# Batch 0's kv taken straight from the loaded v, and batch 2's transposes moved to the DMA engines

## The chip, the cores and the metric

The kernel runs on one NeuronCore of a Trainium2 chip. The core has a matrix engine (TensorE, PE in the profile, with its weight loads shown as PEld), VectorE (DVE), ScalarE (ACT), GpSimd (POOL) and SyncE (SP), each working through a queue of its own in program order, and 16 DMA engines that all queues share. The metric is the device time of one execution in microseconds. Before the change the median of 14 runs was 296.78 us (296.46 to 298.65).

## The reference

Linear attention over 8 batches, 8 heads, 576 rows and a head size of 64, and behind it a feed-forward layer with a Swish of its own slope per column:

```python
def phi(x):
    return np.where(x > 0, x, np.exp(x) - 1.0) + 1.0
q_p, k_p = (phi(q), phi(k))
kv = np.einsum('bhsd,bhse->bhde', k_p, v)
z = np.sum(k_p, axis=2)
num = np.einsum('bhsd,bhde->bhse', q_p, kv)
den = np.einsum('bhsd,bhd->bhs', q_p, z)[..., None] + 1e-06
x = (num / den)                  # heads joined: 4608 rows of 512
h = x @ w_in                     # 512 to 2048
g = h * (1.0 / (1.0 + np.exp(-beta * h)))
out = g @ w_out                  # 2048 to 512
```

All inputs are float32 in memory; the kernel converts to bfloat16 when it loads. The output is float32.

## The kernel before

One batch is one stage. A batch's 576 rows are four blocks of 128 and a tail of 64; the tails of all batches are gathered in `xT_tail` and go through the feed-forward layer together as a ninth batch at the end. The order of all work is written out by hand: each engine executes its instructions in the order in which the program names them.

The attention of a batch b has these steps. `load_k`, `load_q` and `load_v` (L81 to L88) load with conversion from GpSimd's queue. `exp_` (L225, ScalarE), `relu` (L233, VectorE) and `phi` (L240, VectorE) give phi(q) and phi(k) in the tile `qk_p`. `v_copy` (L323) copies v into `vaug`, whose columns past the 64 of a head hold ones, so that one matmul, `kv_mm` (L330), gives kv and the sum z together. `kv_evac` (L346) brings them from the accumulators into block-diagonal tiles `kv_bd`. `q_trans` (L369) transposes phi(q) with TensorE and copies the result into `q_pT`. `num_mm` (L390) multiplies a block of it with kv. `num_norm` (L401) divides by the denominator and leaves the tile `xs`; `x_trans` (L423) transposes that with TensorE into `xT`, by a copy of VectorE or ScalarE. For the batches from `DMA_T` on (`by_dma`, L218) two things are different: `q_trans_dma` (L382) transposes all of phi(q) in one transfer from SyncE's queue, and `num_norm` itself issues a transposing transfer of each `xs` on that queue (L414).

The feed-forward layer of a batch has `h_phase` (L455), which makes h in groups (a column block ff, from row block t0 to t1) with a SiLU on ScalarE after each, and `y_phase` (L513) or `y_phase_wide` (L545), which makes the output. Both take a plan: a table of which attention steps of the next batch stand behind which group. `y_phase_wide(b)` goes through ff 0 to 11 for four row blocks at once (plan indices 0 to 11) and then finishes block after block (12 to 15). `h_last` makes the last four column blocks in other accumulators, with ScalarE steps of the next batch between their matmuls and their SiLUs. Accumulators are of two kinds: four banks `mm` and two double banks `att`.

Batch 0 has its own start, written out at L578 to L661, since everything waits for it. It divides the 576 rows into 9 groups (j) of 64 and places heads 0 to 3 in partitions 0 to 63 and heads 4 to 7 in partitions 64 to 127 (`nine`, `load_nine`). `exp0`, `relu0`, `phi0`, `q_trans0`, `q_out0`, `kv_mm0` and `kv_evac0` are the steps above for this layout; `warm` (L565) issues matmuls whose result isn't used.

Around the second place, batch 2's attention stands in `y_phase_wide(1)` (L705 to L716): phi(k) and phi(q) at index 1, kv at 6, the transposes of q at 7 to 9, num_mm and num_norm at 9 to 13, the transposes of x at 11 to 14 and the tail's in `h_phase(2)`. GpSimd's queue holds the loads of later batches (`load_next`); a load of k or q waits until exp and relu of the batch whose buffer it takes are done.

## Time and profile before

| what | value |
|---|---|
| median of 14 runs | 296.78 us (296.46 to 298.65) |
| profiled execution | 297.56 us |
| its span | 295.7 us, 4721 instructions |
| TensorE busy | 284.4 us (96%) |
| VectorE, ScalarE busy | 126.7 us (43%), 175.1 us (59%) |
| DMA packets | 69206, 36.43 MB, mean 123 GB/s |
| mean granted clock | 0.998 |

The profile is one execution. Line numbers are those of the kernel before. Times within the span count from its start. A row of the timeline has the start, the time taken by the row's instructions together, the engine, the line, the operation, what it writes and reads, the size, the count, and in brackets how long the engine had been idle and what ended that. A row of the waits has the engine and line that waited, what it waited for, the total in us, the number of times and the longest. A row of the DMA issues has what is written and read, the queue, the operation, the count, the size of one and the median time from issue to landing.

### The profile page before, as it was taken

Reading aid. Unit: us, or ns where it says so; the run is one execution under the profiler, and the core shown is the slowest. Engines: PE = TensorE matmul, PEld = TensorE weight load, DVE = VectorE, ACT = ScalarE, POOL = GpSimd, SP = SyncE. Lnnn points to the kernel's source line nnn. Section 1 sums busy time; section 2 is a strip of 40 time slices with the busy share of each in tenths; the row PEclk is TensorE's granted clock in tenths of the full one; section 3 lists DMA queues with packets and bytes.
Section 4 is the critical chain, followed back from the end, with each engine's and each line's share of the span. In section 5 each row is a group of like instructions: output and inputs, shape, how many; then the busy total and the mean of one; then the engine's idle time right before and its main releaser. Section 6 shows DMA issues by size and latency. Waiting matters only on the chain.

```text
span 295.7 us, 4721 instructions
## 1 busy us (share of the span) xinstructions
PE 284.4 (96%) x1876; PEld 144.5 (49%) x1897; DVE 126.7 (43%) x267; ACT 175.1 (59%) x232; POOL 50.8 (17%) x72
## 2 busy tenths in 40 slices
PE   8589999999999999999999999999999999999994
PEld 3357446644555454445444544454445444444443
DVE  4686478504673164616461647154715400110012
ACT  2689796889988780778087907790770077018500
POOL 8825565334006000230020000000000000000000
PEclk9999999999999999999999999999999999999999
DMA  7999999999939943799357255024502400020032
GB/s 104 196 207 345 256 272 191 257 193 190 154 124 162 181 94 100 130 171 150 104 124 82 74 115 125 2 71 115 124 2 72 118 35 0 35 91 17 0 72 72
DMA packets 69206, 36.43 MB, mean 123 GB/s; under 512 B 37808, under 2 KB 63680, under 8 KB 69184
## 3 DMA queue, kind: packets, MB, share of 16 engines
q0 software_dynamic: 38400, 20.45, 47.5%
q1 hardware_dynamic: 30624, 15.55, 20.4%
q8 instruction: 15, 0.25, 0.3%
q10 hardware_dynamic: 160, 0.13, 0.2%
q14 instruction: 7, 0.06, 0.1%
HBM read 36.71 MB, written 9.44 MB: 156 GB/s over the span
## 4 chain that ended last, share of the span: by engine, by line
PE 70%; DMA 22%; ACT 2%; issue 2%; POOL 1%; DVE 0%; POOLq 0%
PE mm L448 33%; PE mm L500 32%; DMA xqk<-in_q_dram 9%; DMA xqk<-in_k_dram 6%; DMA w_in<-in_moe_w_in_dram 4%; DMA vraw<-in_v_dram 4%; PE att L394 2%; PE att L339 1%; PE mm L532 1%; ACT e L228 1%; ACT g L440 1%; POOL xqk L132 1%; POOL w_in L160 0%; ACT L228 0%; ACT L573 0%
## 5 line engine op out<-in xcount | busy, mean ns | idle before, releaser
L440 ACT ACTIVATE g<-mm,beta_c 128x512 bf16<-128x512 f32 (+2 forms) x156 | 97.5, 633 | 88.3 <-PE mm L448 88.1
L500 PE MATMUL mm<-w_out,g 128*128 128x512 bf16 x541 | 127.2, 379 | 1.2 <-issue 0.3
L448 PE MATMUL mm<-xT,w_in 128*128 128x512 bf16 (+2 forms) x560 | 108.0, 349 | 0.8 <-DVE xT L365 0.8
L448 PEld LDWEIGHTS <-w_in 128*128 128x128 bf16 x656 | 62.2, 98 | 61.7 <-issue 1.0
L500 PEld LDWEIGHTS <-g 128*128 128x128 bf16 x560 | 52.8, 98 | 57.3
L510 DVE COPY y_sb<-mm 128x512 f32<-128x512 f32 x27 | 18.7, 691 | 70.6 <-PE mm L500 65.6
L228 ACT ACTIVATE e<-xqk 128x2560 bf16<-128x2560 bf16 x14 | 31.9, 2329 | 0.1
L410 DVE TENSOR_TENSOR xs<-att,rden 128x512 bf16<-128x512 f32 (+1 forms) x40 | 27.6, 689 | 1.4
L241 DVE TENSOR_TENSOR qk_p<-r,e 128x2560 bf16<-128x2560 bf16 x14 | 20.9, 1491 | 14.0 <-ACT e L228 13.4
L350 DVE CAST kv_bd<-att 64x130 bf16<-64x130 f32 x28 | 8.2, 292 | 35.1 <-PE att L339 34.8
L72 POOL DMA_DIRECT2D vraw<-in_v_dram x7 | 6.4, 910 | 77.0 <-DVE vaug L365 71.0
L408 DVE TENSOR_SCALAR den<-att 128x8 f32<-128x8 f32 (+1 forms) x40 | 6.4, 161 | 26.9 <-PE att L394 26.7
L394 PEld LDWEIGHTS <-q_pT 128*128 128x128 bf16 (+1 forms) x160 | 11.7, 100 | 10.4 <-DVE xs L410 2.1
L394 PE MATMUL att<-kv_bd,q_pT 128*128 128x130 bf16 (+1 forms) x160 | 15.8, 221 | 0.7 <-DVE kv_bd L365 0.4
L448 PE MATMUL mm<-xT_tail,w_in 128*128 128x512 bf16 x63 | 13.9, 379 | 0.1
L236 DVE TENSOR_SCALAR r<-xqk 128x2560 bf16<-128x2560 bf16 x14 | 11.8, 848 | 4.0 <-DMA xqk<-in_q_dram 2.5
L567 PE MATMUL mm<-g 128*128 128x512 bf16 x35 | 9.8, 434 | 1.2 <-DVE g L144 1.2
L228 ACT ACT_TABLE_LOAD x7 | 9.0, 1283 | 0.1
L409 DVE RECIPROCAL rden<-den 128x8 f32<-128x8 f32 (+1 forms) x40 | 8.1, 201 | 1.4
L72 POOL DMA_DIRECT2D xqk<-in_k_dram x7 | 6.2, 890 | 10.7 <-ACT e L228 5.3
L255 ACT ACTIVATE e<-xqk 128x1280 bf16<-128x1280 bf16 (+1 forms) x4 | 4.4, 1157 | 6.1 <-DMA xqk<-in_k_dram 6.0
L72 POOL DMA_DIRECT2D xqk<-in_q_dram x7 | 6.6, 940 | 8.4 <-DMA xqk<-in_k_dram 5.4
(72 smaller groups left out, 142.9 us busy)
## 6 DMA issues: line engine op xcount, KB each, us to landing
out_dram<-y_sb SPq DMA_DIRECT2D x28, 256.0 KB, 2.3
xqk<-in_k_dram POOLq DMA_DIRECT2D x7, 512.0 KB, 10.8
xqk<-in_q_dram POOLq DMA_DIRECT2D x7, 512.0 KB, 12.4
vraw<-in_v_dram POOLq DMA_DIRECT2D x7, 512.0 KB, 11.6
w_in<-in_moe_w_in_dram POOLq DMA_DIRECT2D x4, 512.0 KB, 10.1
g<-in_moe_w_out_dram POOLq DMA_DIRECT2D x4, 512.0 KB, 10.7
out_dram<-y_sb SPq DMA_DIRECT2D x14, 128.0 KB, 5.2
xqk<-in_moe_w_out_dram POOLq DMA_DIRECT2D x2, 512.0 KB, 13.7
```

What stands on the lines that cost most here:

```text
L72: eng.dma_start(out=dst[:, :, 0:NJ, :].rearrange("p h j d -> p h (j d)"), in_=src[b, :, 0:MAIN, :].rearrange("h (p j) d -> p h (j d)", j=NJ),)
L228: nc.scalar.activation(st[b, "e", a][:, h0:h1], xqk[b % NX][:, a, h0:h1], ACTF.Exp)
L236: nc.vector.tensor_scalar(st[b, "r", a][:, h0:h1], xqk[b % NX][:, a, h0:h1], 0.0, 1.0, ALU.max, ALU.add)
L241: nc.vector.tensor_tensor(st[b, "p"][:, a].rearrange("p j (h d) -> p h j d", h=H)[:, h0:h1], st[b, "r", a][:, h0:h1], st[b, "e", a][:, h0: ...
L350: nc.vector.tensor_copy(kv_bd[b % 2][i][gs, :, g, :], st[b, "kvp"][gs, 2 * i : 2 * i + 2, :])
L394: nc.tensor.matmul(nps[:n, p // 2, c0 : c0 + 2 * (D + 1)], st[b, "qT"][:, t, p, :n], kv_bd[b % 2][p // 2][:, p % 2], start=True, stop=True ...
L410: nc.vector.tensor_mul(xs[:n], nv[:, :, :, 0:D], rden[:n, :, :, None].to_broadcast([n, 2, 4, D]))
L440: nc.scalar.activation(g_sb[b % 2][:, ff, c0:c1], hp[:, c0:c1], ACTF.Silu, scale=beta_c[:, ff : ff + 1],)
L448: nc.tensor.matmul(hp[:, c0:c1], w_in_sb[ff // 4][:, kc, (ff % 4) * P : (ff % 4 + 1) * P], x[:, t0:t1, kc, :] if b < B else x[:, kc, c0:c1 ...
L500: nc.tensor.matmul(yp, g_sb[b % 2][:, ff, t * P : (t + 1) * P], w_out_sb[ff // 4][:, ff % 4, :], start=(ff == 0), stop=(ff == FC - 1),)
L510: nc.vector.tensor_copy(y_sb, yp)
L567: nc.tensor.matmul(st["warm"], g_sb[0][:, FC - 1, 0:P], g_sb[0][:, FC - 1, :], start=True, stop=True, skip_group_check=True,)
```

## The change

In batch 0, kv_mm0 takes v as it was loaded, without the copy and its column of ones. The sums z are made by matmuls of their own, which multiply phi(k) with a tile of two columns of ones and write one column per head of the same accumulators. The loads of v are divided by row group (j below 6, then the rest) instead of by head. phi(q) of the later row groups is made in two pieces, the third q block is transposed before the first h groups, and the others, with their copies, move to other places of the plan and partly from VectorE to ScalarE. `DMA_T` becomes 2, so batch 2's phi(q) and its attention output are transposed by DMA. In batch 2, exp, relu and phi of q come before those of k, and the transfer is issued between phi of q and phi of k. `h_phase(2)` begins with six column blocks in halves (row blocks 0 and 1, then 2 and 3) instead of four.

```diff
-    DMA_T = 3
+    DMA_T = 2
...
-    load_nine(v9, v, h1=2)
-    load_nine(v9, v, h0=2)
+    load_nine(v9, v, j1=6)
+    load_nine(v9, v, j0=6)
...
-    nc.vector.memset(va9[:, :, :, D : D + 2], 1.0)
-    set_ones(1)
+    for i in range(2):
+        set_ones(i)
+    ones = consts.tile([P, 2], BF16)
+    nc.vector.memset(ones, 1.0)
...
-    def v_copy0(h0, h1):
-    def kv_mm0(a, kvp):
...
+    def kv_cols(kvp, g, a):
+        m0 = a * 2 * (D + 1)
+        return kvp[g][:, m0 : m0 + 2 * (D + 1)].rearrange("p (i e) -> p i e", i=2)
+
+    def kv_mm0(kvp, j0, j1, of_v):
+        for j in range(j0, j1):
+            for a in range(2):
+                for g in range(2):
+                    gs = slice(g * TAIL, (g + 1) * TAIL)
+                    cols = kv_cols(kvp, g, a)
+                    nc.tensor.matmul(
+                        cols[:, :, 0:D] if of_v else cols[:, :, D],
+                        st["p0"][1][gs, j, 2 * a : 2 * a + 2, :],
+                        v9[gs, 2 * a : 2 * a + 2, j, :] if of_v else ones[gs],
...
     phi0(0, 0, 4)
-    v_copy0(0, 2)
+    kvp = [mm_bank([P, 512]) for _ in range(2)]
+    kv_mm0(kvp, 0, N9, False)
     qb = att_banks(BF16)
     q_trans0(0, qb, 0)
     q_trans0(1, qb, 256)
-    kvp = [mm_bank([P, 512]) for _ in range(2)]
-    kv_mm0(0, kvp)
     q_out0(0, qb, 0, False)
     q_out0(1, qb, 256, False)
-    warm(1)
-    v_copy0(2, HH)
-    kv_mm0(1, kvp)
+    kv_mm0(kvp, 0, 6, True)
+    kv_mm0(kvp, 6, N9, True)
     kv_evac0(kvp)
...
     num_norm(0, 0)
+    phi0(0, 4, 6)
     warm(4)
     x_trans(0, 0, dve=True)
-    phi0(0, 4, N9)
+    qb2 = att_banks(BF16)
+    q_trans0(2, qb2, 0)
+    q_out0(2, qb2, 0, False)
     num_norm(0, 1)
+    phi0(0, 6, N9)
...
+    def q_rest0():
         q_trans0(3, qb2, 256)
-        q_out0(2, qb2, 0, False)
-        st["qb2"] = qb2
+        q_trans0(4, qb2, 512)
+        q_out0(3, qb2, 256, False)
+        q_out0(4, qb2, 512, False)
...
-            1: [F(q_second)],
-            3: [F(x_trans, 0, 1, dve=True), F(num_mm, 0, 2), F(num_norm, 0, 2),
-                lambda: q_out0(3, st["qb2"], 256, False)],
+            3: [F(x_trans, 0, 1), F(num_mm, 0, 2), F(num_norm, 0, 2), F(q_rest0)],
             5: [F(num_mm, 0, 3), F(num_norm, 0, 3)],
-            6: [F(q_tail0)],
             7: [F(x_trans, 0, 2)],
-            9: [F(x_trans, 0, 3)],
-            10: [F(num_mm, 0, 4), F(num_norm, 0, 4), F(tidy0)],
-            14: [F(x_trans, 0, 4)],
+            8: [F(num_mm, 0, 4), F(num_norm, 0, 4)],
+            9: [F(x_trans, 0, 3), F(tidy0)],
+            12: [F(x_trans, 0, 4)],
...
-            8: [F(begin, 2), F(relu, 2, 1)],
-            10: [F(relu, 2, 0)],
+            8: [F(begin, 2), F(relu, 2, 0)],
+            10: [F(relu, 2, 1)],
...
-    h_last(1, xT[1], [F(exp_, 2, 1), F(exp_, 2, 0)])
+    h_last(1, xT[1], [F(exp_, 2, 0), F(exp_, 2, 1)])
...
-        1: [F(phi, 2, 1), F(phi, 2, 0)],
+        1: [F(phi, 2, 0), F(q_trans_dma, 2), F(phi, 2, 1)],
         6: [F(kv_mm, 2), F(kv_evac, 2)],
-        7: [F(q_trans, 2, 0, 1, wide=True, dve=True)],
-        8: [F(q_trans, 2, 2, 3, wide=True, dve=True)],
-        9: [F(q_trans, 2, 4, wide=True, dve=True), F(num_mm, 2, 0), F(num_norm, 2, 0)],
+        9: [F(num_mm, 2, 0), F(num_norm, 2, 0)],
         10: [F(num_mm, 2, 1), F(num_norm, 2, 1)],
-        11: [F(num_mm, 2, 2), F(num_norm, 2, 2), F(x_trans, 2, 0, wide=True)],
-        12: [F(num_mm, 2, 3), F(num_norm, 2, 3), F(x_trans, 2, 1, wide=True)],
-        13: [F(num_mm, 2, 4), F(num_norm, 2, 4), F(x_trans, 2, 2, wide=True)],
-        14: [F(x_trans, 2, 3, wide=True)],
+        11: [F(num_mm, 2, 2), F(num_norm, 2, 2)],
+        12: [F(num_mm, 2, 3), F(num_norm, 2, 3)],
+        13: [F(num_mm, 2, 4), F(num_norm, 2, 4)],
...
-                [(ff, 0, 2) for ff in range(4)] + [(ff, 2, 4) for ff in range(4)] + ALL[4:]
+                [(ff, 0, 2) for ff in range(6)] + [(ff, 2, 4) for ff in range(6)] + ALL[6:]
             )
-            plan = {1: [F(x_trans, 2, 4)]}
```

## The prediction

> **What bounds the kernel now.** I read the page's busy times and slices first, then TensorE's idle times, then the order of time around the two places that the diff touches, and last the DMA issues. Busy times and slices of the page before:
>
> ```profile
> PE 284.4 (96%) x1876; PEld 144.5 (49%) x1897; DVE 126.7 (43%) x267; ACT 175.1 (59%) x232; POOL 50.8 (17%) x72
> ...
> DMA  7999999999939943799357255024502400020032
> ```
>
> TensorE (PE) is the bound: what leaves its queue is gained, what makes it wait is lost. The DMA row is saturated for about the first 11 slices of 7.4 us, to about 81 us. TensorE's idle times are short; the first belongs to batch 0's start, the second to ScalarE's copies in batch 2:
>
> ```profile
> PE att L281 <- DVE qk_p L269: 2.5, 1, 2.5
> ...
> PE att L394 <- ACT xT L367: 0.3, 1, 0.3
> ```
>
> Batch 0's start, TensorE in order of time. The two rows of L304 are the kv matmuls; between them TensorE waits for the second copy of v:
>
> ```profile
> 12.26 0.41 PE L281 MATMUL att<-identity,qk_p 64*128 64x64 bf16 x16 [2.53 <-DVE qk_p L269]
> 12.63 0.69 PE L304 MATMUL mm<-vaug,qk_p 64*128 64x130 bf16 x18
> 13.58 0.69 PE L304 MATMUL mm<-vaug,qk_p 64*128 64x130 bf16 x18 [0.25 <-issue]
> ```
>
> Batch 2's attention, TensorE; the rows of L375 and L428 are the transposes that the change hands to the DMA engines:
>
> ```profile
> 73.91 0.82 PE L339 MATMUL att<-vaug,qk_p 128*64 128x65 bf16 x40
> 74.89 0.81 PE L500 MATMUL mm<-w_out,g 128*128 128x512 bf16 x3 [0.16 <-issue]
> 75.54 0.61 PE L375 MATMUL att<-identity,qk_p 128*128 128x128 bf16 x8
> 75.98 1.03 PE L500 MATMUL mm<-w_out,g 128*128 128x512 bf16 x4
> ...
> 78.47 0.40 PE L394 MATMUL att<-kv_bd,q_pT 128*128 128x130 bf16 x4
> ...
> 81.19 0.40 PE L428 MATMUL att<-identity,xs 128*128 128x128 bf16 x4
> ...
> 86.69 1.04 PE L448 MATMUL mm<-xT,w_in 128*128 128x256 bf16 x8
> ```
>
> The DMA issues of the page. The 128 KB stores take over twice as long as the 256 KB ones; eight of the fourteen are batch 0's, issued at 49 to 54 us beside the loads (5.2 to 5.6 us each there). The q transposes of batches 3 to 7 take 4.9 us on a queue that is nearly empty:
>
> ```profile
> out_dram<-y_sb SPq DMA_DIRECT2D x28, 256.0 KB, 2.3
> ...
> out_dram<-y_sb SPq DMA_DIRECT2D x14, 128.0 KB, 5.2
> ...
> q_pT<-qk_p SPq DMA_TRANSPOSE x5, 4.9
> ```
>
> **Part A, batch 0.** Both v copies leave VectorE (0.69 and 0.45 us, 12.13 to 13.24 us). The 36 kv matmuls then follow the 16 transposes without a gap: pairs at 0.057 us in the rows above, so 18 pairs from 12.63 us end at 13.8 instead of 14.27 us, 0.45 us earlier. They need the v loads: issued from 4.70 us, 5.6 to 6 us to landing each, so the last at about 12.45 us, before the matmuls of j 6 to 8 at 13.3 us. The 36 new sum matmuls, two columns each, start at phi(k)'s first half (10.4 us); only the last 16 come after its second half at 11.53 us. At the 0.015 us of a 64-row transpose they end at 11.8, at an unpaired 0.06 us at 12.5 us; phi(q) releases the transposes at 12.21 us, so their price is 0 to 0.3 us, taken as 0 since the 64-row transposes are the nearest form. The memsets (0.12 us each) move to where VectorE waits for the first load; one warming matmul of 0.22 us goes.
>
> The two v loads per half become longer and shorter rows, 512 more packets for the same bytes on GpSimd's queue, ahead of the second half of q, w_in and everything after. The DMA rate is 200 GB/s at 882 bytes a packet (9 to 17 us) and about 190 at 365 (66 to 80 us), so 0.6 MB costs 0.15 us more; bounds 0 and 0.7. Its cover: q's second half lands at 14.1 us and its exp starts at 14.5 (before 14.92), the first w_in lands at 16.7 and its matmul starts at 17.1 (before 17.55). At 0.7 us both covers are gone and Part A with them.
>
> The next steps inherit the 0.45 us: evacuation 14.30 to 13.85, num_mm, den, xs, the first transposed x. phi(q) of j 4 to 8 (0.81 us) is cut into 0.36 us, beside the transposes of x, and 0.5 us after the second normalisation, which so starts about 0.8 us sooner. Against it, ScalarE takes over the copies of x block 1 and of q block 4 (0.60 and 0.38 us, from VectorE) and q block 2 ahead of its SiLUs. I walked the three queues on with the durations of the page (SiLU 0.31 and 0.43, copies 0.5, four bank buffers): block 1's h starts at 19.6 to 19.8 instead of 20.24 us, the first 512-wide h group 0.45 to 0.75 us earlier than its 28.1 us. I take -0.6 us, bounds -0.9 and 0 (ScalarE late, or the loads). What is late next: v of batch 1 lands at 41.55 us and kv_mm of batch 1 stands at 43.78 us, with its copy of 0.99 us between: slack 0.6 us after the shift.
>
> **Part B, TensorE's work in batch 2.** From 74.89 to 86.69 us pass 11.80 us. Left are nine steps of four 512-wide matmuls (0.863 each, 7.77) and five num_mm (0.235, 1.17): 8.94. Gone are 2.86 us, the 0.29 us wait for ScalarE among them, and 0.22 us of the tail's transposes at 87.66 us; eight more matmul starts in the six plus six half groups cost 0.03. Sum -3.05 us. Copies gone: 1.67 us of VectorE, five of ScalarE (0.6 each); cover for nothing needed. relu and exp only change order.
>
> **Part B, the new wait.** exp of q starts first on ScalarE (66.52 us, 2.3 us), phi(q) runs at 68.89 to 70.38 us on VectorE, and SyncE, empty since 54.6 us, issues the transpose at 70.4 us (3.0 us of its queue, then 4.9 to landing from issue: 75.3 us). First use is num_mm at 73.91 + 0.98 + 3 x 0.863 = 77.48 us. With an empty DMA queue it lands 2.2 us early. The queue is not empty: v of batch 4 and k and q of batch 5 follow one another to 80.8 us (busy nines in 66 to 80 us). Moreover k of batch 5 now waits for the later exp, 71.1 instead of 69.15 us, still before v is through at 74.2 us. Two readings of the batch-0 stores price it. A 128 KB store took 5.3 us where an undisturbed 256 KB one takes 2.3, so 3.0 us pass before its turn: landing at 78.3. Then stores and loads shared the engines at about half each, 236 GB/s together: the transpose's own 3.0 us (saturated from 121.4 to 124.4 us for batch 4) become 6.0: landing 81.3. If it were served after all loads: 83.8. If nothing disturbed: 75.3. I take 81.3, as the stores are the only case of SyncE's queue against full loads. Part A moves need and issue up by 0.6 us, the landing (half of it loads) by about 0.3: wait 81.0 - 76.9 = 4.1 us, bounds 0 and 7.
>
> Behind num_mm in TensorE's queue stands the rest of batch 1's output, so all of the 4.1 us is idle time. VectorE's normalisations follow at 1.1 us each as before, and the five x transposes (2.3 to 2.6 us to landing) then meet a nearly empty queue; blocks 2 and 3 have six half groups (2.6 us) of cover. On SyncE each takes 1.2 us of the queue; the fourth and fifth stand behind stores of 0.3 to 0.5 us that wait for ScalarE's copies, which its freed 3 us now bring early; the q transpose of batch 3 (issued at 88.1 us, used at 103.5) stands behind them with 10 us to spare. Nothing on GpSimd is moved but the load of k. After such an idle time the clock may be lower: the first ten 512-wide matmuls of the kernel took 3.92 us where twenty later ones took 4.49, but after 2.5 us idle (before 12.26 us) matmuls were at full rate. So 0 to 2 us, taken as 0.6.
>
> On DMA the Trainium skill (DMA: Bandwidth & Descriptors, Queues, rings and completion order) says each engine serves its rings in turn, packet by packet; by that rule the transpose's small packets would get less than the half that the stores got, landing nearer 83. It says also that any transposing beside ordinary DMAs needs nothing, which is of safety and not of time. On the clock (TensorE: Matmul & The Clock Gate, Part 1) an idle window of about 3.4 us halves the rate for about as long, an estimated 1.7 us; the idle 2.5 us in this trace is too short to show it.
>
> **Sum.** -0.6 - 3.05 + 4.1 + 0.6 = +1.05 us. The profiled execution took 297.56 us (span 295.7 and 1.9 around), 0.78 above the median of 296.78; taken from the median: 297.8 us.
>
> **Rivals.** (1) The transpose is served soon enough, landing before 77.5: nothing but its own 4.9 us row speaks for it, the stores' 5.2 against. Then x transposes 0 and 1 meet the delayed loads and cost some 0.6 us: 296.78 - 0.6 - 3.05 + 0.6 = 293.7. It decides at a landing of about 80: up to there the gain outweighs the wait. (2) It is served last: wait 7, clock 1: 296.78 - 3.65 + 8 = 301.1. For it, the transpose's packets are a fifth of the loads' size. (3) Part A gives nothing as the short v rows or ScalarE hold it: each case 0.6 higher. (4) Only the start delay of 3 us, no sharing: wait 1.2: 294.4.
>
> **How the numbers follow.** Late by half sharing 0.38 (295.8 to 299.8), served last 0.22, in time 0.22, start delay alone 0.18. The likeliest is 297.8. Leaving out a tenth at each end of all cases gives 293.4 to 301.0. A change under 0.2% (0.6 us) is about what measuring can't tell from none: under 296.2 lie (1), (4) and a little of the first, 0.42; over 297.4 (2) and most of the first, 0.47; between, 0.11.
>
> **What would show it.** Right: no copies of v, and the kv matmuls of v starting within 0.2 us after the 16 transposes; h's first group near 17.1 us; in 74 to 90 us one idle stretch of TensorE of about 4 us before L394, released by the DMA of q_pT, whose time to landing is about 11 us against 4.9 for later batches. Wrong: that landing under 7.5 us and no idle time; or a slower clock over many microseconds; or TensorE waiting for xT at the head of batch 2's h.

## The result, and the profile after

The changed kernel takes 303.22 us in the median (302.23 to 304.81, ten runs), the kernel before 296.85 us (296.46 to 298.65, 47 runs): a ratio of 1.0217, with a 95% interval of 1.0204 to 1.0231. It is slower by 6.4 us, beyond the 301.0 us at which the forecast's range ended. The profiled execution of it took 305.02 us (span 303.2, clock 0.981), 1.8 us over its median, so the trace shows the loss somewhat larger than it usually is.

The slices of TensorE before, and then the busy times and slices of the page after. In the rows of digits each digit is one of 40 slices of the span (7.4 us before, 7.6 us after): the row PE is TensorE's busy share in tenths, the row PEclk the granted clock in tenths of full speed.

```profile
PE   8589999999999999999999999999999999999994
```

```profile
PE 285.1 (94%) x1879; PEld 144.8 (48%) x1900; DVE 123.3 (41%) x261; ACT 173.4 (57%) x231; POOL 53.5 (18%) x72
...
PE   8789999999179999999999999999999999999994
...
PEclk9999999999859999999999999999999999999999
DMA  7999999999985995299429143314321610010023
```

TensorE was in constant use before but for the start; now its eleventh slice has a 1, and the clock falls to 8 and 5 tenths in the eleventh and twelfth. The waits of TensorE after name the reason in their first line (released by the DMA that writes q_pT, 8.2 us in total, once, 8.2 us the longest):

```profile
PE att L399 <- DMA q_pT<-qk_p: 8.2, 1, 8.2
PE mm L572 <- DVE g L143: 1.2, 1, 1.2
```

Batch 2's attention on TensorE in order of time, after. It is the stretch that ran from 73.91 to 86.69 us before, with its transposes:

```profile
73.55 0.82 PE L344 MATMUL att<-vaug,qk_p 128*64 128x65 bf16 x40
74.53 2.54 PE L505 MATMUL mm<-w_out,g 128*128 128x512 bf16 x11 [0.16 <-issue]
85.25 0.61 PE L399 MATMUL att<-kv_bd,q_pT 128*128 128x130 bf16 x4 [8.19 <-DMA q_pT<-qk_p]
85.66 1.91 PE L505 MATMUL mm<-w_out,g 128*128 128x512 bf16 x4
87.37 0.64 PE L399 MATMUL att<-kv_bd,q_pT 128*128 128x130 bf16 x4
...
91.38 1.02 PE L505 MATMUL mm<-w_out,g 128*128 128x512 bf16 x4
...
94.42 0.82 PE L453 MATMUL mm<-xT,w_in 128*128 128x256 bf16 x6
```

Three things can be read here. The work taken away is really gone: between kv and h stand only num_mm (L399) and the rest of batch 1's output. num_mm waits 8.19 us for the transposed q, twice what was forecast. And the four output matmuls behind the wait take 1.91 us where they take 1.02 us from 91.38 us on: the clock is at half speed from 80.4 to 90.6 us, and TensorE works in the last 5.4 us of that. The table of stretches agrees (after the stretch and its length come the busy time and count of TensorE's matmuls, of its weight loads, of VectorE, ScalarE and GpSimd, then the clock, the DMA share and GB/s):

```profile
74.00:78.00 4.00, 2.91 (x35) 1.35 (x30) 1.17 (x4) 3.97 (x3) 0.14 (x1) 1.00 1.45 121
78.00:82.00 4.00, 0.00 (x0) 0.00 (x0) 0.00 (x0) 3.82 (x4) 0.00 (x0) 0.80 1.52 141
82.00:86.00 4.00, 0.75 (x5) 0.56 (x6) 0.10 (x1) 0.00 (x0) 0.00 (x0) 0.50 1.46 170
86.00:90.00 4.00, 4.00 (x17) 1.98 (x16) 2.03 (x6) 0.00 (x0) 0.00 (x0) 0.50 0.54 60
```

The DMA issues of k and q of batch 5 before, with what one takes to landing, and then those between 66 and 90 us after:

```profile
xqk<-in_k_dram POOLq DMA_DIRECT2D x1, 512.0 KB, 8.1
xqk<-in_q_dram POOLq DMA_DIRECT2D x1, 512.0 KB, 8.5
```

```profile
xqk<-in_k_dram POOLq DMA_DIRECT2D x1, 512.0 KB, 15.1
xqk<-in_q_dram POOLq DMA_DIRECT2D x1, 512.0 KB, 16.6
...
q_pT<-qk_p SPq DMA_TRANSPOSE x1, 15.1
```

So the transfer was late, and it made the loads it met late too. In the table of stretches the engines carry only 121 and 141 GB/s from 74 to 82 us, where both run, against about 190 for the loads alone, as in the same stretch before:

```profile
74.00:78.00 4.00, 3.84 (x67) 2.59 (x68) 2.36 (x6) 3.97 (x4) 0.00 (x0) 1.00 1.58 192
```

Batch 0's start after, in order of time, shows the first part in place: sums as soon as phi(k) is there, and the 36 kv matmuls right behind the transposes.

```profile
11.41 0.35 PE L307 MATMUL mm<-ones,qk_p 64*128 64x2 bf16 x16 [0.80 <-DVE qk_p L270]
12.01 0.41 PE L282 MATMUL att<-identity,qk_p 64*128 64x64 bf16 x16 [0.25 <-DVE qk_p L270]
12.26 1.18 PE L307 MATMUL mm<-vraw,qk_p 64*128 64x128 bf16 x36
...
16.90 1.05 PE L453 MATMUL mm<-xT,w_in 128*128 128x128 bf16 x16 [0.29 <-DVE xT L370]
```

One caution for what follows: the first load of k landed at 6.6 to 7.5 us in the profiled executions of all the experiments, but at 8.2 and 7.9 us in the two of before and after, so that batch 0's start stands up to 1.6 us later in those two traces.

### The profile page after: what moved, and what is told of

It is laid out like the page before. It is cut to its first block, busy times and chain, and to the rows that moved or that the text cites. A ratio compares the mean times of both kernels' runs of the same rounds, so it can differ in the third digit from the quotient of the medians.

```text
span 303.2 us, 4737 instructions
## 1 busy us (share of the span) xinstructions
PE 285.1 (94%) x1879; PEld 144.8 (48%) x1900; DVE 123.3 (41%) x261; ACT 173.4 (57%) x231; POOL 53.5 (18%) x72
## 4 chain that ended last, share of the span: by engine, by line
PE 83%; DMA 7%; ACT 5%; DVE 2%; issue 2%; POOL 0%; ACTq 0%; DVEq 0%; POOLq 0%
PE mm L453 39%; PE mm L505 35%; DMA q_pT<-qk_p 5%; PE att L399 3%; PE att L453 2%; DMA xqk<-in_k_dram 2%; ACT e L229 2%; PE att L344 1%; PE mm L537 1%; ACT e L256 1%; ACT L578 1%; ACT q_pT L372 1%; ACT g L445 1%; DVE qk_p L242 0%; PE mm L433 0%
## 5 line engine op out<-in xcount | busy, mean ns | idle before, releaser
L505 PE MATMUL mm<-w_out,g 128*128 128x512 bf16 x541 | 129.0, 383 | 1.2 <-issue 0.3
L453 PEld LDWEIGHTS <-w_in 128*128 128x128 bf16 x664 | 62.9, 98 | 60.7 <-issue 0.5
L505 PEld LDWEIGHTS <-g 128*128 128x128 bf16 x560 | 53.5, 99 | 59.0 <-issue 1.6
L242 DVE TENSOR_TENSOR qk_p<-r,e 128x2560 bf16<-128x2560 bf16 x14 | 20.9, 1490 | 13.1 <-ACT e L229 12.4
L399 PE MATMUL att<-kv_bd,q_pT 128*128 128x130 bf16 (+1 forms) x160 | 16.5, 228 | 9.0 <-DMA q_pT<-qk_p 8.2
L399 PEld LDWEIGHTS <-q_pT 128*128 128x128 bf16 (+1 forms) x160 | 12.2, 103 | 19.5 <-DMA q_pT<-qk_p 8.7
L513 ACT ACTIVATE y_sb<-mm 128x512 f32<-128x512 f32 x8 | 4.8, 597 | 13.0 <-PE mm L505 13.0
```

The costliest lines, as they stand in the source:

```text
L242: nc.vector.tensor_tensor(st[b, "p"][:, a].rearrange("p j (h d) -> p h j d", h=H)[:, h0:h1], st[b, "r", a][:, h0:h1], st[b, "e", a][:, h0: ...
L399: nc.tensor.matmul(nps[:n, p // 2, c0 : c0 + 2 * (D + 1)], st[b, "qT"][:, t, p, :n], kv_bd[b % 2][p // 2][:, p % 2], start=True, stop=True ...
L453: nc.tensor.matmul(hp[:, c0:c1], w_in_sb[ff // 4][:, kc, (ff % 4) * P : (ff % 4 + 1) * P], x[:, t0:t1, kc, :] if b < B else x[:, kc, c0:c1 ...
L505: nc.tensor.matmul(yp, g_sb[b % 2][:, ff, t * P : (t + 1) * P], w_out_sb[ff // 4][:, ff % 4, :], start=(ff == 0), stop=(ff == FC - 1),)
```

## The experiments

**The two parts alone.** `a_only` is the changed kernel with batch 2 as before; `b_only` is the kernel before with batch 2 as changed. The first one's edit:

```diff
-    DMA_T = 2
+    DMA_T = 3
-        1: [F(phi, 2, 0), F(q_trans_dma, 2), F(phi, 2, 1)],
+        1: [F(phi, 2, 1), F(phi, 2, 0)],
...
```

> Only batch 0's part; batch 2 is transposed by TensorE as before. Theory (batch 0's part gains about 1.0 us by the first 512-wide h group, and 0.6 us of it are given back where batch 1's copy of v waits for its load): 0.3 to 0.5 us faster than before, h of batch 0 starting near 16.9 us and TensorE's kv_mm of batch 2 near 73.5 instead of 73.9 us. Rival (batch 0's part is worth nothing, or slower, and all of the loss is not batch 2's alone): no change or slower.

> Only batch 2's part; batch 0 starts as before. Theory (the whole loss is batch 2's: the wait for phi(q)'s transpose of 8.2 us and the slower clock after it, against 3.0 us of TensorE's work): 6.6 to 7.0 us slower than before, a wait of 8 us for q_pT, landing 15 us after issue. Rival (batch 0's part shifts the loads against the transpose and makes it land late): wait under 5 us, under 3 us slower.

Measured: batch 0's part alone 296.80 us (ratio 1.0000, 0.9991 to 1.0008), batch 2's part alone 302.10 us (1.0183, 1.0165 to 1.0201). So batch 2's part alone loses 5.4 of the 6.4 us, less than the 6.6 to 7.0 expected, and batch 0's part, forecast at -0.6 us, is worth nothing: there the rival was right. The remaining 1.0 us appears only where both parts are together. In `b_only` the transfer took 13.1 us and the wait is shorter than in the changed kernel; why it lands later with the changed batch 0 is not shown.

```profile
PE att L394 <- DMA q_pT<-qk_p: 6.2, 1, 6.2
```

**Taking the loads out of the transfer's way.** In `hold5` k and q of batch 5 are loaded only after batch 2's phi(q) has been transposed: GpSimd, which issues the loads, first copies two columns of the transposed tile. `hold4` holds back v of batch 4 too.

The edit of `hold5`, and then that of `hold4`, which has the copy too:

```diff
+    def hold():
+        nc.gpsimd.tensor_copy(held, st[2, "qT"][:, 0, 0, 0:2])
...
-        1: [F(phi, 2, 0), F(q_trans_dma, 2), F(phi, 2, 1)],
+        1: [F(phi, 2, 0), F(q_trans_dma, 2), F(phi, 2, 1), F(hold)],
```

```diff
-            12: [F(v_copy, 2), F(load_next, 4)],
+            12: [F(v_copy, 2), F(load_k, 4), F(load_q, 4)],
...
-        1: [F(phi, 2, 0), F(q_trans_dma, 2), F(phi, 2, 1)],
+        1: [F(phi, 2, 0), F(q_trans_dma, 2), F(phi, 2, 1), F(hold), F(load_v, 4)],
```

> The changed kernel with one small GpSimd copy of q_pT ahead of the loads of batch 5, so that these loads start only when the transpose has landed. Theory (the transpose shares the DMA engines with k and q of batch 5, and both are served slowly): only the rest of v of batch 4 is in its way; landing 7 to 9 us after issue instead of 15.1, wait 0 to 1.5 us, clock at full rate, 293 to 294.5 us. Rival 1 (the 3 us start delay and the transpose's own slowness in this place make the 15 us, not the loads of batch 5): landing at 12 us or more, 300 us or more. Rival 2 (what the loads lose, compute loses later): wait gone and another wait for k, q or v of batch 5.

> As the run with the loads of batch 5 held, and v of batch 4 held too, so that at the issue only q of batch 4 is in the queue (to about 72 us). Theory (loads in the queue are the whole delay): landing 5 to 6.5 us after issue, no wait for q_pT, 292 to 293.5 us. Rival (an empty queue is not enough): landing over 8 us and a wait that stays.

Measured: 303.15 us (1.0214, 1.0192 to 1.0236) and 300.94 us (1.0140, 1.0125 to 1.0154), some 9 and 7 us above what was expected. The time to landing of the q transfer falls from 15.1 to 9.3 and to 5.2 us, and its wait from 8.2 to 2.4 us and to none. What came in its place stands in the waits of `hold5` and `hold4`, in this order:

```profile
PE mm L453 <- DMA xT<-xs: 3.3, 1, 3.3
PE att L399 <- DMA q_pT<-qk_p: 2.4, 1, 2.4
```

```profile
PE mm L453 <- DMA xT<-xs: 4.7, 2, 4.3
```

The loads that were let go now met the transposes of x, which took 7.6 and 8.2 us to landing (2.5 in the next kernel). So it is the loads that delay the transposes, whichever they meet, and moving them by a few microseconds moves the collision. In `hold5` each of the two waits, 2.4 and 3.3 us, was also followed by 3.4 us at half clock; behind the first:

```profile
79.44 1.46 PE L505 MATMUL mm<-w_out,g 128*128 128x512 bf16 x4
81.12 1.91 PE L505 MATMUL mm<-w_out,g 128*128 128x512 bf16 x4
```

**Only the x transposes by DMA.** `a_x` is the changed kernel with batch 2's phi(q) transposed by TensorE, as before, and only its x by DMA. These are issued when the loads are through.

```diff
-        1: [F(phi, 2, 0), F(q_trans_dma, 2), F(phi, 2, 1)],
+        1: [F(phi, 2, 0), F(phi, 2, 1)],
+        7: [F(q_trans, 2, 0, 1, wide=True, dve=True)],
+        8: [F(q_trans, 2, 2, 3, wide=True, dve=True)],
+        9: [F(q_trans, 2, 4, wide=True, dve=True), F(num_mm, 2, 0), F(num_norm, 2, 0)],
```

> The changed kernel with batch 2's phi(q) transposed by TensorE again; its attention output is still transposed by DMA. Theory (only the transfer of phi(q) is harmful, as it is needed 7 us after issue in a full queue; the x transposes are needed later): no wait for q_pT, TensorE saves the x transposes (1.35 us) and the 0.3 us wait, 1.5 to 2.0 us faster than before. Rival (the x transposes meet the loads of batch 5 until 81 us and land late, so TensorE waits for xT at the head of h of batch 2): gain under 0.7 us or a loss.

Measured: 295.03 us (0.9945, 0.9932 to 0.9957), 1.7 us under before. The x transposes land as they do for later batches:

```profile
xT<-xs SPq DMA_TRANSPOSE x4, 2.5
```

That is the forecast's "then meet a nearly empty queue", true here, where q is not in the way. It is the same change, less one transfer, and it is faster than before.

**The clock.** `warm` is the changed kernel with 36 matmuls, whose result isn't used, in the place of the wait.

```diff
-        9: [F(num_mm, 2, 0), F(num_norm, 2, 0)],
+        9: [F(warm_wait, 36), F(num_mm, 2, 0), F(num_norm, 2, 0)],
```

> The changed kernel with 36 matmuls of unused result (36 x 0.215 = 7.7 us) ahead of batch 2's first num_mm, in the time in which TensorE waits for q_pT. Theory (of the 6.4 us, some 2.9 are the clock, which is halved after the 8 us of idle time): the wait for landing stays, landing unchanged, but 512-wide matmuls after it start 0.216 us apart instead of 0.43; 2.5 to 3 us faster than the changed kernel, about 300.3 us. Rival (the slow matmuls after the wait are something else, as the DMA's traffic): same time as the changed kernel.

Measured: 301.94 us (1.0179, 1.0164 to 1.0195), 1.3 us under the changed kernel. The timeline of `warm` at the same place:

```profile
76.97 7.93 PE L572 MATMUL att<-g 128*128 128x512 bf16 x36
84.74 0.39 PE L399 MATMUL att<-kv_bd,q_pT 128*128 128x130 bf16 x4
84.97 1.02 PE L505 MATMUL mm<-w_out,g 128*128 128x512 bf16 x4
```

Now 1.02 us stands directly behind the wait, and from the first num_mm to h pass 6.6 us where the changed kernel needs 9.2. So the slow matmuls come from the idle time and not from the traffic, and in the traces the idle time costs 2.6 to 2.8 us of clock. In the medians it is 1.3 us, half of what was expected. Two things on record lie between. The 36 matmuls hold num_mm back until 84.7 us, 0.5 us after q_pT has landed. And the changed kernel does not always lose as much as in its trace: its executions with a granted clock of 0.987 to 0.989 took 302.2 to 303.4 us, those with 0.980 to 0.982, the profiled one among them, 304.2 to 305.0 us (two with 0.985 took 302.9 and 304.0).

The traces show when the clock falls. In all 18 of them its changes lie whole multiples of 3.41 us apart. Divided into such stretches, from the first change at 4 to 7 us on up to 285 us, there are eight at full clock in which TensorE had 1.8 to 3.4 us of idle time, and behind each of them the clock was halved; behind all others at full clock, with at most 1.6 us, it was not. So the 2.5 us of batch 0's start before the change, which fall into two stretches (1.6 us in the first), left the clock as it was, and the 2.4 us in `hold5`, all in one stretch, halved it. In `a_x` and `warm` several short waits of batch 0's start add up to 1.8 us in one stretch, and the clock is halved from 17.6 to 21 us.

**The transfer in pieces.** `split` transposes phi(q) by row block, five transfers for one.

```diff
+        if b == 2:
+            for t in range(NT):
+                nc.sync.dma_start_transpose(
+                    out=st[b, "qT"][:, t], in_=st[b, "p"][:, 0, t]
+                )
+            return
```

> The changed kernel with batch 2's phi(q) transposed in five transfers, one per row block, so that the first num_mm needs only the first. Loads of batch 5 are in the queue as in the changed kernel. Theory (start delay of 3 us, then service shared with the loads): the first block lands 6 to 8 us after issue and the rest some 2 us apart, so TensorE's idle time falls to 2 to 5 us in pieces under 3 us each, the clock stays up, 296 to 299 us. Rival (the transfers wait for one another or for the loads as a whole): the first block lands after 12 us or more, and the time stays over 301 us.

Measured: 298.96 us (1.0071, 1.0057 to 1.0086). The first block lands 6.4 us after issue, in time, the last at 86.5 us, later than the single transfer's 85.2; but TensorE has work in between, and the longest of its waits is 3.0 us:

```profile
PE att L405 <- DMA q_pT<-qk_p: 3.5, 2, 3.0
```

The last block lands no earlier than the whole did; the blocks are only waited for one by one. The time is in the expected range, but the clock did not stay up as expected: from 81.9 us, behind the 3.0 us, it is halved for 3.4 us.

**The loads out of the way of both.** In `paced_ab` v of batch 4 and k and q of batch 5 wait until batch 3's phi(q) is transposed, that is until after both kinds of batch 2's transposes, and the later batches' loads follow at the same pace. `paced_b` is the same with batch 0 as before the change.

```diff
-            12: [F(v_copy, 2), F(load_next, 4)],
+            12: [F(v_copy, 2), F(load_k, 4), F(load_q, 4)],
...
-            plan[3 + o] = [F(relu, n, 0), F(phi, n, 0), F(q_trans_dma, n)]
+            plan[3 + o] = [F(relu, n, 0), F(phi, n, 0), F(q_trans_dma, n), F(hold, n)]
...
-        load_next(b + 3)
+        if b + 2 < B:
+            load_v(b + 2)
+        if b + 3 < B:
+            load_k(b + 3)
+            load_q(b + 3)
```

> The changed kernel, but v of batch 4 and k and q of batch 5 are loaded only after batch 3's phi(q) has been transposed (GpSimd copies two columns of it ahead of them), and later batches' loads follow in the same step, so that both kinds of transposes of batch 2 meet an empty DMA queue. Theory (the only thing wrong with the second part is that its transposes meet the loads of later batches): no wait for q_pT and none for xT in batch 2, q_pT lands about 5 us after its issue, and the 3.05 us of TensorE's work taken away show in full: 293.3 to 294.2 us, 2.6 to 3.5 us under before and 1 to 1.7 us under the version with TensorE's phi(q) transposes and DMA's x transposes (295.0). Rival (the loads were early for a reason; postponed, they collide with batch 3's transposes or come late for its kv): a new wait for v or k of batch 4 or 5, or for xT of batch 3, and 295.5 us or more.

> The same pacing of the loads with the second part alone, batch 0 as before. Theory (batch 0's part is worth nothing, since the loads of q, w_in and v of batch 1 bind there): within 0.5 us of the paced kernel with both parts. Rival (batch 0's part is worth the 0.6 us that was forecast): 0.6 us or more slower than that one.

Measured: 294.20 us (0.9914, 0.9898 to 0.9931) and 293.81 us (0.9898, 0.9886 to 0.9911). Both beat the kernel before, by 2.6 and 3.0 us, and the changed kernel by 9.0 and 9.4 us. They differ by 0.4 us in the wrong direction for batch 0's part, with intervals that overlap. In the trace of `paced_ab` the first x transpose of batch 3, issued at 101.5 us, meets the postponed loads and takes 8.2 us to landing, and TensorE waits for it:

```profile
PE mm L453 <- DMA xT<-xs: 0.6, 1, 0.6
```

In `paced_b` it takes 6.4 us and isn't waited for. The timeline of `paced_b`, from kv to h of batch 2:

```profile
73.53 0.82 PE L339 MATMUL att<-vaug,qk_p 128*64 128x65 bf16 x40
74.51 2.54 PE L500 MATMUL mm<-w_out,g 128*128 128x512 bf16 x11 [0.16 <-issue]
76.88 0.39 PE L394 MATMUL att<-kv_bd,q_pT 128*128 128x130 bf16 x4
77.12 1.02 PE L500 MATMUL mm<-w_out,g 128*128 128x512 bf16 x4
...
83.44 0.82 PE L448 MATMUL mm<-xT,w_in 128*128 128x256 bf16 x6
```

No wait, no slow clock: 9.91 us where the kernel before takes 12.78, so 2.87 us are gone here. To batch 3's kv pass another 11.37 instead of 11.68 us. The DMA issues of `paced_b` from 69 to 77 us, with the rate of each 0.2 us, show the transfer alone on the engines from 71.4 us on, at about 215 GB/s:

```profile
GB/s 200 200 181 174 154 107 74 60 51 28 19 33 197 221 216 210 206 223 209 220 225 209 220 223 211 219 202 45 0 0 0 0 0 0 0 0 0 0 0 0
...
q_pT<-qk_p SPq DMA_TRANSPOSE x1, 5.0
```

**Why batch 0's part gives nothing: two attempts.** `a_relu` is `a_only` with relu of q's second half behind the first normalisation on VectorE (it had waited there for q); `a_v` is `a_only` with batch 1's kv and the copy of its v later.

```diff
-    relu0(0, 4, N9)
     silu_table()
     num_norm(0, 0)
+    relu0(0, 4, N9)
```

```diff
+    phi(1, 0)
     v_copy(1)
-    phi(1, 0)
...
-        9: [F(kv_mm, 1), F(kv_evac, 1), F(w_out_scale, 3)],
-        10: [F(q_trans, 1, 0, 1, wide=True), F(q_trans, 1, 2, 3, wide=True)],
+        9: [F(q_trans, 1, 0, 1, wide=True)],
+        10: [F(kv_mm, 1), F(kv_evac, 1), F(w_out_scale, 3), F(q_trans, 1, 2, 3, wide=True)],
```

> Batch 0's part alone, with relu of the second half of q moved behind the first normalisation on VectorE, where it had stood ahead of it and waited for the load of q. Theory (behind that wait the first w_in binds, which lands at 16.5 to 16.8 us): xs is 0.5 to 0.8 us earlier, h of batch 0 begins at the same time within 0.2 us, and the time is that of batch 0's part alone, 296.8 us within 0.3. Rival (the relu is what kept the gain back): h of batch 0 begins 0.5 us earlier or more, and the time is 296.3 us or less.

> Batch 0's part alone, with batch 1's kv (and the copy of its v) moved one group later, and two of its transposes of phi(q) put ahead of it. Theory (half a microsecond gained within batch 0's h is lost again where batch 1's kv waits for v, which lands at 41.9 us): the wait of TensorE for the copy of v, 0.5 us, is gone, and the time is 0.4 to 0.6 us less than batch 0's part alone: 296.2 to 296.4 us. Rival (nothing is gained within batch 0 but by chance of the start): 296.8 us within 0.2.

Measured: `a_relu` 296.92 us (1.0000, 0.9988 to 1.0012), a time as the theory had it. In its trace w_in lands at 17.1 us, later than the 16.5 to 16.8 of the theory, h of batch 0 begins at 17.2 us, and the wait ahead of it is for the first w_in:

```profile
PE mm L453 <- DMA w_in<-in_moe_w_in_dram: 0.8, 1, 0.8
```

`a_v` came out at 298.34 us (1.0058, 1.0044 to 1.0072), a miss for both sides. The 0.5 us wait for v is gone, but the later kv put waits of 0.3 us (w_out's scaling) and 0.6 us (xs) behind it, in the 0.9 us that batch 1's attention is now longer. The move cost more than the wait, and says nothing of batch 0.

**v of batch 1 out of the way.** `half_before` and `half_a` are the kernel before and `a_only`, with 0.5 MB of w_out not loaded ahead of v of batch 1 (another part is used in its place).

```diff
-        for ii in range(2):
+        for ii in range(1 if i == 2 else 2):
```

> The kernel before, with half of one quarter of w_out (0.5 MB) not loaded (the other half is used twice), so that v of batch 1, which stands behind it in GpSimd's queue, lands some 2.5 us earlier, near 39.4 us. Theory (v of batch 1 is what holds the time of batch 1 in the versions with batch 0's part): in the kernel before v is hardly waited for, so little changes here, 296.2 to 296.8 us; the size of batch 0's part is read from the next run against this one. Rival: the same here.

> Batch 0's part alone, with the same half quarter of w_out left unloaded. Theory (batch 0's h runs 0.5 us shorter with that part, and the gain is lost only where v of batch 1 lands at 41.9 us and its copy, phi of q and the kv copies follow on VectorE): with v early, batch 1's h begins 0.4 to 0.7 us earlier than in the kernel before with the same omission, and the time is 0.4 to 0.7 us less than that one's. Rival (something else in batch 1 takes the gain, or there is none): within 0.2 us of that one.

Measured: 296.67 us (0.9993, 0.9984 to 1.0001) and 296.50 us (0.9996, 0.9982 to 1.0010). v of batch 1 lands at 40.4 and 40.8 us, about 1 us earlier and not 2.5. The wait for v is gone in both and batch 1 runs alike in both (8.73 us from its first output matmul to kv, 8.9 on to h), yet batch 0's part is worth 0.2 us at most. The theory of v alone is refuted. In `half_a` h of batch 0 begins at 16.93 us, after a wait for w_in, in `half_before` at 16.34 us without one:

```profile
PE mm L453 <- DMA w_in<-in_moe_w_in_dram: 1.1, 1, 1.1
```

The landing events of the first w_in, one for each of the 16 DMA engines, read from the trace:

| kernel | 15th engine, us | 16th engine, us | first transfer of instructions, us |
|---|---|---|---|
| half_before | 15.98 | 15.99 | 17.32 |
| b_only | 15.64 | 15.69 | 17.62 |
| paced_b | 15.85 | 15.88 | 17.62 |
| half_a | 15.72 | 16.89 | 14.83 |
| a_only | 15.94 | 16.52 | 14.41 |
| a_relu | 16.54 | 17.12 | 15.04 |
| a_v | 15.74 | 17.00 | 14.72 |

With the changed batch 0 one engine is 0.6 to 1.3 us late in these four. In the other kernels with it and all its sums the sixteenth engine is 0.4 to 1.0 us behind the fifteenth, but 0.1 us in the trace of the changed kernel itself, whose k came late. The profile's table of DMA queues from 9 to 17 us has a line in `half_a` that `half_before` has not (packets, MB, share of the 16 engines' time):

```profile
q8 instruction: 1, 0.02, 0.7%
```

0.7% of 16 times 8 us is 0.9 us: one packet of 16 KB that held one engine for 0.95 us. The profile names it as the program's own instructions. TensorE has issued about the same count of weight loads at that moment in either kind, 128 and 135. The guess that follows is that the transfer goes by TensorE's place in its program, and that the 36 added sum matmuls bring that place forward by 3 us; the next runs test it.

**The instruction transfer.** `short_half` is `half_a` with four of the 36 sum matmuls, `short_a` the same with all of w_out loaded, `long_half` is `half_before` with 36 unused matmuls of two columns in the idle start, for two warming ones.

```diff
-    kv_mm0(kvp, 0, N9, False)
+    kv_mm0(kvp, 0, 1, False)
```

```diff
-    warm(20)
+    warm(18)
+    for _ in range(36):
+        nc.tensor.matmul(st["warm"][0:TAIL, 0:2], g_sb[0][0:TAIL, FC - 1, 0:TAIL], ...)
```

> Batch 0's part with half of a quarter of w_out unloaded, and of the 36 sum matmuls only the four of row group 0 (so the sums z of batch 0 leave out eight of nine row groups). Theory (the 36 added matmuls bring TensorE's first transfer of instructions, 16 KB that hold one DMA engine for 0.95 us, from 17.3 to 18.5 us in the kernels with the old batch 0 forward to 14.4 to 15.8 us, where it stands ahead of that engine's share of the first w_in; this engine alone lands it 0.6 to 1.2 us after the others, and h of batch 0 waits for it): that transfer goes back behind 16.3 us, the first w_in lands by 16.1 us on all engines, h of batch 0 begins at 16.1 to 16.4 instead of 16.93 us, and the time is 0.4 to 0.8 us less than with all 36 sums: 295.7 to 296.1 us. Rival (w_in is late for the shorter rows of v, as the forecast's bound had it): w_in lands at 16.8 us as before, and the time stays at 296.5 within 0.2.

> The same four sum matmuls, with all of w_out loaded. Theory: h of batch 0 begins 0.4 us earlier or more than with all 36, but kv of batch 1 then waits for v, which lands at 41.9 us whatever batch 0 does, so that batch 1's h begins at 52.0 to 52.3 us as ever, and the time is 296.5 to 296.8 us: both loads, the first w_in and v of batch 1, stand in the way, one behind the other. Rival (v of batch 1 binds only by chance): as much gained as with half a quarter of w_out unloaded, 296.1 us or less.

> The kernel before with half of a quarter of w_out unloaded, and 36 unused matmuls of two columns put in the idle start in place of two warming ones. Theory: TensorE's first transfer of instructions comes forward to 14 to 15.5 us, the first w_in then lands 0.6 to 1.2 us late on one engine, h of batch 0 begins at 16.8 to 17.1 instead of 16.34 us, and the time is 0.3 to 0.7 us more than the 296.67 us without them. Rival: w_in lands at 16.0 us, and the time is the same within 0.2.

| kernel | median, us | ratio to before | instruction transfer | w_in lands | h of batch 0 | h of batch 1 |
|---|---|---|---|---|---|---|
| half_before | 296.67 | 0.9993 (0.9984 to 1.0001) | 17.32 | 15.99 | 16.34 | 51.49 |
| long_half | 296.79 | 1.0002 (0.9987 to 1.0017) | 14.86 | 16.91 | 16.95 | 51.66 |
| half_a | 296.50 | 0.9996 (0.9982 to 1.0010) | 14.83 | 16.89 | 16.93 | 51.58 |
| short_half | 295.81 | 0.9972 (0.9958 to 0.9986) | 15.72 | 15.89 | 16.27 | 51.06 |
| short_a | 296.94 | 1.0003 (0.9989 to 1.0016) | 15.83 | 16.09 | 16.51 | 51.95 |

Adding matmuls to the old batch 0 makes w_in 0.9 us late; taking them from the new one puts it right, with the new, shorter rows of v still there. That settles the cause of the late w_in: the instruction transfer, not the rows. How the transfer's time follows from the program is less clear: in `long_half` TensorE had issued 134 weight loads by then, as the guess has it, but 111 in `short_half` and 107 in `short_a`. The transfer in `short_half`, at 15.72 us, is so earlier than was expected, but w_in's last part was nearly through by then. Of the times, `long_half` fell short of the theory: h begins 0.6 us late and only 0.1 to 0.2 us of it are left at batch 1, since the old order has idle time inside batch 0's h that takes up part of the rest (in the first 4 us of h 0.5 us in `half_before`, 0.2 in `long_half`). `short_a`, at 296.94 us, came out 0.1 us above what the theory gave, and far from the rival's 296.1: with v of batch 1 where it is, the gain of `short_half` is lost again. Its VectorE, in order of time, shows v awaited by the copy, and phi of q and the kv copies following it without a pause:

```profile
41.76 0.83 DVE L370 COPY vaug<-vraw 128x2560 bf16<-128x2560 bf16 x1 [0.38 <-DMA vraw<-in_v_dram]
42.50 1.49 DVE L242 TENSOR_TENSOR qk_p<-r,e 128x2560 bf16<-128x2560 bf16 x1
43.90 1.20 DVE L355 CAST kv_bd<-att 64x130 bf16<-64x130 f32 x4
```

So batch 0's part, with most of its sums left out, has an edge of 0.6 to 0.7 us by the ratios of `short_half` against `half_before` and `half_a` (0.4 to 0.5 us at h of batch 1 in the traces; the left-out sums stand ahead of an idle 1.2 us of TensorE). Two loads, one behind the other, both keep it from being paid out.

## Why the prediction was wrong

The account of the traces of before and after, to batch 3's kv: batch 2's kv starts 0.36 us earlier; the wait adds 8.19; the work gone is 2.87 + 0.31 = 3.18; and the stretch from kv to h is 20.87 us, which less the wait and less `paced_b`'s 9.91 leaves 2.77 us for the slow clock. -0.36 + 8.19 - 3.18 + 2.77 = +7.42 us, and batch 3's kv stands 7.43 us later (98.37 to 105.80).

**TensorE's work in batch 2, -3.05 us.** Right. 3.18 us in the trace; 2.99 us in the median of `paced_b`, where nothing stands against it.

**The new wait, 4.1 us with bounds 0 and 7.** The mechanism was right, the q transfer is late behind the loads of batches 4 and 5, and the size was wrong: 8.19 us, beyond the upper bound. The issue was right (70.1, forecast 70.4 us), and the need about (TensorE waits from 77.1 us, forecast 76.9). What lies between issue and landing can be set beside the same transfer on empty engines in `paced_b` (times from the packets of the two traces, in us):

| step of the q transfer | alone, `paced_b` | changed kernel | longer by | forecast to be longer by |
|---|---|---|---|---|
| issue to first packet | 1.3 | 3.1 | 1.8 | 3.0 |
| first to last packet | 3.2 | 9.3 | 6.1 | 3.0 |
| last packet to landing | 0.5 | 2.7 | 2.2 | 0 |
| issue to landing | 5.0 | 15.1 | 10.1 | 6.0 |

The step that failed is "stores and loads shared the engines at about half each, 236 GB/s together", by which the transpose's own 3.0 us became 6.0: its packets took 9.3 us, and another 2.7 us passed until the last engine had landed its part (13 of the 16 had by 83.3 us, the others at 84.0, 84.3 and 85.2 us, and TensorE waits for the last). It was not the "about half each": from 74 to 80 us the transposes moved 0.47 MB and the loads 0.26. It was the total of 236 GB/s, taken from the stores of batch 0. Here the two moved 122 GB/s together in these 6 us, where the loads alone move 190 and the transpose alone 215. For the same reason the bound of 7 us was no bound: "served after all loads" took the loads to end at 80.8 us, and they ended 8 us later. The start delay was the one part taken too long, 3.0 us more than undisturbed for 1.8.

The stores were the only row of that queue against full loads, but in the trace they are packets of 2 KB that hold an engine for 96 ns, longer than the 60 ns of the loads' 512 bytes, where the transposes' are of 256 bytes and, alone, 18 ns; this could be seen beforehand. (Rival (2) has the transpose's packets as a fifth of the loads' size; the loads' are of 512 and 128 bytes, 371 on average.) What the mixing did to both can be counted: from 76 to 80 us 809 transposing packets moved, at a median of 75 ns in the first half and 52 in the second, and some 430 of the loads' 512-byte packets, of which some 640 went in every 2 us before.

On this the Trainium skill (DMA: Bandwidth & Descriptors, Queues, rings and completion order) has each engine serve its rings in turn by the packet; the forecast worked out a landing near 83 us from it and set it aside for the stores. The trace's 85.2 is nearer to that, but not for its reason, that small packets would get less than half: from 74 to 80 us they got nearly two thirds of the bytes, 1852 packets against 637.

**The clock, 0.6 us within 0 to 2.** Too small: 2.77 us in the trace, and at least the 1.3 us between the medians of `warm` and the changed kernel. Its size hung on the length of the wait. That the 2.5 us of idle time in batch 0's start left the rate alone was no guide: what counted in the traces was the idle time within one of the stretches of 3.41 us. Three of these went by at half clock, from 80.4 to 90.6 us, with 5.4 us of work in them, which so took 2.7 us longer. The rule of the Trainium skill (TensorE: Matmul & The Clock Gate, Part 1), estimated at 1.7 us, was nearer than the forecast to the trace, and still below.

**The x transposes meeting an empty queue.** Right in the changed kernel, where they come after everything because they are late, and in `a_x`; wrong once q is in time (`hold5`, `hold4`): then they meet the loads (7.6 and 8.2 us to landing). This was a second collision behind the first, and the forecast's rival (1) had priced it at 0.6 us where 4.7 us were seen, so that 293.7 us needed the loads out of the way of both, as in `paced_ab` with 294.2.

**Batch 0, -0.6 us, bounds -0.9 and 0.** Its step by step walk to the kv matmuls holds (with k equally late or equally early they end 0.6 to 0.8 us earlier), but the sum is 0. Rival (3) foretold it, with a reason that does not hold: `short_half` has the short rows of v, and its w_in lands at 15.89 us; and TensorE waits there for ScalarE's copies 0.5 us in all, with the gain still there. The covers named, the first w_in at 16.7 and q at 14.1 us, were measured in an execution whose k came late; relative to the work they bind as soon as k is in time (w_in is waited for up to 1.1 us). The added matmuls had been costed at nothing on TensorE, which was right, and their 3 us earlier transfer of instructions was not thought of. The "late next", v of batch 1, was named with a slack of 0.6 us; in executions with k in time the slack is nil (`a_only` waits 0.5 us for the copy of it).

**What was to show it.** The one idle stretch of TensorE before L394, "released by the DMA of q_pT", came true, with 8.2 for 4 us and 15.1 for 11 us to landing. So did the kv matmuls right behind the transposes and h near 17.1 us (16.9). Of the signs of being wrong one came too: "a slower clock over many microseconds".

## What to carry to other kernels

Before work is moved from a busy engine to the DMA engines, look at what they carry at that moment: with the loads out of the way of batch 2's transposes the kernel took 294.2 us, with the transposes beside the loads 303.2 us, so move the loads or leave the transfer. When two kinds of transfer meet, do not assume that the sum of the rates is kept, and do not take the price from transfers with packets of another size. A gain is only paid out where nothing behind it is as late, so look up each load's landing in more than one execution before calling it cover, and count added instructions as transfers too.

## What the runs showed of the hardware that was not expected

- 256-byte transposing packets beside converting loads: together 121 to 141 GB/s in the changed kernel (stretches of 4 us from 74 to 82 us; 144 and 158 in `b_only`), where the loads alone move 190 and the transposes alone 215. A transfer that takes 5.0 us to landing took 13.1 to 15.1, and the loads that it met, in the changed kernel, 15.1 and 16.6 instead of 8.1 and 8.5 us. Why the mixture is so slow was not found out.
- TensorE's clock in the 18 traces changes only at whole multiples of 3.41 us from another change. At full clock a stretch of that length with 1.8 us or more of idle time was followed by half clock each time (eight cases), one with 1.6 us or less never. So 2.4 us of waiting halved the rate in `hold5`, and 2.5 us, spread over two stretches, did not in the kernel before.
- The larger transfers of instructions are of 16 KB, the first of them one packet that holds one DMA engine for 0.95 us. Where the first such packet stood ahead of w_in, mostly one engine of 16 landed its share 0.4 to 1.3 us late, and the load with it; 36 matmuls more or less of TensorE decided where it fell.
